# RetNet attention into a SiLU feed-forward block on one core: SiLU as one ScalarE operation, a shorter float64 conversion, an undecayed state, and a new order of the first and last groups

## Chip, core and metric

The kernel runs on one core of a Trainium2 chip. The metric is the device time of one execution in microseconds (us); lower is better. The engines are TensorE (PE, with its weight loads as PEld), VectorE (DVE), ScalarE (ACT), GpSimd (POOL) and SyncE (SP), whose queue issues nearly all DMAs.

## Reference

```python
# q, k, v: (4, 8, 768, 64) float32; w_in: (512, 2048), w_out: (2048, 512), float64
gamma = 1.0 - 2.0 ** (-5.0 - np.arange(H))
for t in range(S):
    state = gamma * state + einsum('bhd,bhe->bhde', k[:, :, t], v[:, :, t])
    y[:, :, t] = einsum('bhd,bhde->bhe', q[:, :, t], state) / sqrt(D)
x = y.transpose(0, 2, 1, 3).reshape(3072, 512)
h = x @ w_in
out = (h / (1 + exp(-h))) @ w_out          # SiLU, then the second product
```

## The kernel before

The sequence is cut into 6 **groups** `c` of 128 positions. A **unit** is the attention of one of the 4 batches in one group, with all 8 heads: 24 units in all. A unit has four stages. `stage_t` loads ahead, scales q (DVE, `qs`) and v (POOL, `vs`) by powers of gamma and transposes k and q on PE. `stage_a` makes the scores `sc` in two sets of 64-row matmuls (`j` = 0, 1, one for each half of the partitions) and masks them (`am`). `stage_y` adds the part from earlier groups (`y<-qt,state`) and the part from this group (`y<-am,vs`) in PSUM and splits the result into three fp32r parts of `xt`. `stage_s` makes the group's state update `s`, adds it to `state` and multiplies by the group's decay `gc`. The state of a head pair is kept as a 128x128 block with zeros off its diagonal, so that `y<-qt,state` has 128 rows of contraction and 64 output columns.

A **product** `product_in(c, f)` is one of 16 column blocks `f` of the first matrix product for group `c`: 12 matmuls of 512 columns into `ha` and `hb`; ACT scales `ha` into `hs` (L322), DVE subtracts `hb` (L323), ACT takes the sigmoid (L325), POOL multiplies (L326), and the result `g` goes to DRAM. PSUM holds two products at a time.

The weights are float64 in DRAM. `convert_w` makes float32 of them with integer operations on DVE: 8 per block (L158 to L173), of which five read one tensor and three read two. A block of `w_in` is then split in three (`split_w`: two ACT and two DVE operations); a converted block of `w_out` goes back to DRAM and is read and split later. `take_w` does one block.

Order of the first part: the units of group 0 with four blocks taken; then for each group all 16 products, each followed by one stage of the next group's attention. Group 0 takes a block after every product, the groups after it after one product in four. The second part (L409 to L411) then has 6 groups of 192 matmuls; its 16 blocks of `w_out` are read and split in its first group, two blocks ahead (`S_AHEAD`).

The calls are arranged on each engine's queue when the program is built; each queue then runs in that order, and an engine waits at its next instruction.

Of the kernel before, what the change touches and what calls it, by code (L numbers as in the profile page):

```python
# [12 lines left out]
FP32 = mybir.dt.float32  # L13
# [18 lines left out]
def kernel(  # L32
# [20 lines left out]

    nc = tc.nc
# [9 lines left out]
    assert S % C == 0 and NF == 4 * B  # L64
# [6 lines left out]
    dram = ctx.enter_context(tc.tile_pool(name="dram", bufs=1, space=bass.MemoryType.DRAM))  # L71
    wpool = ctx.enter_context(tc.tile_pool(name="wpool", bufs=1))
# [7 lines left out]
    def split_w(pool, f, w32, name):  # L80

        w = wpool.tile([128, 3, 512], FP32R, tag=f"w{f}", name=f"{name}{f}")
        lo = pool.tile([128, 512], FP32, tag="wl", name=f"{name}l_{f}")
# [9 lines left out]
    with ExitStack() as first:  # L93
        const = first.enter_context(tc.tile_pool(name="const", bufs=1))
        ld = first.enter_context(tc.tile_pool(name="ld", bufs=2))
        one = first.enter_context(tc.tile_pool(name="one", bufs=1))
        work = first.enter_context(tc.tile_pool(name="work", bufs=2))
        stage = first.enter_context(tc.tile_pool(name="stage", bufs=2))
        conv = first.enter_context(tc.tile_pool(name="conv", bufs=1))
        gp = first.enter_context(tc.tile_pool(name="gp", bufs=3))  # L100
        ps_a = first.enter_context(tc.tile_pool(name="ps_a", bufs=4, space=PS))
        ps_h = first.enter_context(tc.tile_pool(name="ps_h", bufs=2, space=PS))

        units = [(c, b) for c in range(NC) for b in range(B)]
        loaded = {}

        def load(n):
            if n >= len(units):
                return
            c, b = units[n]  # L110
            tiles = []
            for name, src in (("q", q), ("k", k), ("v", v)):
                t = ld.tile([128, H, D], FP32, tag=f"{name}f", name=f"{name}f_{n}")
                nc.sync.dma_start(out=t, in_=src[b, :, ds(c * C, C)].rearrange("h t d -> t h d"))
                tiles.append(t)
            loaded[n] = tiles
# [3 lines left out]
        staged = {}  # L120

        def load_w(i):
            if i >= 2 * NF:
                return
            if wide:
                t = stage.tile([128, 2 * DM], U32, tag="wf", name=f"wf_{i}")
                w_in, w_out, n = moe_w_in.bitcast(U32), moe_w_out.bitcast(U32), 256
            else:
                t = stage.tile([128, DM], FP32, tag="wf", name=f"wf_{i}")
                w_in, w_out, n = moe_w_in, moe_w_out, 128  # L130
            if i < NF:
                nc.sync.dma_start(out=t.rearrange("p (i f) -> p i f", i=KIN),
                                  in_=w_in[:, ts(i, n)].rearrange("(i p) f -> p i f", p=128))
            else:
                nc.sync.dma_start(out=t, in_=w_out[ts(i - NF, 128), :])
            staged[i] = t

        def convert_w(i):

            load_w(i + W_AHEAD)
            t = staged.pop(i)
            if not wide:  # L150
                return t
            words = t.rearrange("p (c w) -> p c w", w=2)
            lo, hi = words[:, :, 0], words[:, :, 1]
            a = conv.tile([128, DM], U32, tag="ca", name=f"ca_{i}")
            s = conv.tile([128, DM], U32, tag="cs", name=f"cs_{i}")
            p = conv.tile([128, DM], U32, tag="cp", name=f"cp_{i}")
            w = conv.tile([128, DM], FP32, tag="cw", name=f"cw_{i}")
            nc.vector.tensor_scalar(out=a, in0=hi, scalar1=0x7FFFFFFF, scalar2=None,  # L158
                                    op0=ALU.bitwise_and)
            nc.vector.tensor_scalar(out=a.bitcast(FP32), in0=a.bitcast(FP32),  # L160
                                    scalar1=bits((1151 << 20) - 1), scalar2=bits(896 << 20),
                                    op0=ALU.min, op1=ALU.max)
            nc.vector.tensor_scalar(out=a, in0=a, scalar1=4, scalar2=0x80000000,
                                    op0=ALU.logical_shift_left, op1=ALU.bitwise_xor)
            nc.vector.tensor_scalar(out=a, in0=a, scalar1=1, scalar2=None,
                                    op0=ALU.logical_shift_right)
            nc.vector.scalar_tensor_tensor(out=s, in0=hi, scalar=0x80000000, in1=a,  # L167
                                           op0=ALU.bitwise_and, op1=ALU.bitwise_or)
            nc.vector.tensor_scalar(out=p, in0=s, scalar1=0xFF800000, scalar2=None,
                                    op0=ALU.bitwise_and)  # L170
            nc.vector.scalar_tensor_tensor(out=p.bitcast(FP32), in0=lo, scalar=2.0 ** -52,
                                           in1=p.bitcast(FP32), op0=ALU.mult, op1=ALU.mult)
            nc.vector.tensor_tensor(out=w, in0=s.bitcast(FP32), in1=p.bitcast(FP32), op=ALU.add)  # L173
            return w

        w_sb = {}

        def take_w(i):
            if i >= 2 * NF:
                return  # L180
            w32 = convert_w(i)
            if i < NF:
                w_sb[i] = split_w(conv, i, w32, "wi")
            else:
                nc.sync.dma_start(out=wo_dram[i - NF], in_=w32)

        AHEAD = 2
        W_AHEAD = 2
        for n in range(max(AHEAD, W_AHEAD)):
            load(n)  # L190
            load_w(n)

        pos = const.tile([128, 1], FP32, tag="pos", name="pos")
        nc.gpsimd.iota(pos, pattern=[[0, 1]], base=1, channel_multiplier=1,
                       allow_small_or_imprecise_dtypes=True)
        ident = const.tile([128, 128], FP32, tag="ident", name="ident")
        make_identity(nc, ident)
        mask = const.tile([128, C], FP32, tag="mask", name="mask")
        nc.vector.memset(mask, 1.0)
        nc.gpsimd.affine_select(out=mask, in_=mask, compare_op=ALU.is_ge, fill=0.0,  # L200
                                base=0, pattern=[[1, C]], channel_multiplier=-1)
        lgp = const.tile([128, H], FP32, tag="lgp", name="lgp")
        for h in range(H):
            nc.vector.tensor_scalar(out=lgp[:, h : h + 1], in0=pos, scalar1=float(lg[h]),
                                    scalar2=None, op0=ALU.mult)
        gq = const.tile([128, H], FP32, tag="gq", name="gq")
        gk = const.tile([128, H], FP32, tag="gk", name="gk")
        nc.scalar.activation(out=gq, in_=lgp, func=AF.Exp)
        nc.scalar.activation(out=gk, in_=lgp, func=AF.Exp, scale=-1.0)
        nc.vector.tensor_scalar(out=gq, in0=gq, scalar1=scale, scalar2=None, op0=ALU.mult)  # L210
        gc = const.tile([128, HP, 1], FP32, tag="gc", name="gc")
        for a in range(HP):
            for j in range(2):
                nc.vector.memset(gc[ts(j, D), a, :], math.exp(C * lg[2 * a + j]))
        state = [const.tile([128, HP, 128], FP32, tag=f"state{b}", name=f"state{b}")
                 for b in range(B)]
        for st in state:
            nc.gpsimd.memset(st, 0.0)

        xt = {}  # L220
        live = {}

        def bank(name):
            return ps_a.tile([128, 512], FP32, tag="a", name=name)

        def stage_t(n):
            load(n + AHEAD)
            qf, kf, vf = loaded.pop(n)
            qs = one.tile([128, H, D], FP32, tag="qs", name=f"qs_{n}")
# [6 lines left out]
            for name, src in (("k", kf), ("q", qs)):  # L236
                tp = bank(f"{name}tp_{n}").rearrange("p (a t) -> p a t", a=HP)
                for a in range(HP):
                    nc.tensor.transpose(tp[:, a, :], src[:, 2 * a : 2 * a + 2, :], ident)
# [207 lines left out]
```

## Time and profile before

| | |
|---|---|
| median of 3 runs | 767.16 us (766.26 to 768.3) |
| the profiled execution | 766.99 us, of which the span from first to last instruction is 765.3 us |
| PE, PEld busy | 691.3 us (90%), 545.6 us (71%) |
| DVE, ACT, POOL busy | 518.8 (68%), 268.8 (35%), 159.9 us (21%) |
| granted PE clock | 0.953 of full speed over the span |
| DMA | 101.37 MB, 132 GB/s over the span |

A share is an average over parts of the kernel with different limits, so the parts are read apart. A busy PE says that a matmul was under way, not that PE ran at its best.

### The profile page before, as it was taken

The page shows a single profiled execution, that of the slowest core. Times are in us where ns is not written, and L with a number is a line of the kernel's source. Part 1 is how long each engine was busy: PE and PEld are TensorE (multiplying, and loading weights), DVE is VectorE, ACT ScalarE, POOL GpSimd, SP SyncE. Part 2 cuts the span into 40 slices and gives each one's busy share as a digit, 9 for nine tenths or more (in the row PEclk, how much of TensorE's full clock was granted, in tenths as well). Part 3 has the DMA queues.
Part 4 walks back from the last instruction along what each step waited for, and adds up shares of the span by engine and source line. Part 5 has one row for each costly group of instructions (what it writes and reads, how often), then busy time and mean ns, then how long its engine had stood idle before and what let it go on. Part 6 is the DMA issues. An engine that isn't in the chain of part 4 may idle for free.

```text
span 765.3 us, 10695 instructions
## 1 busy us (share of the span) xinstructions
PE 691.3 (90%) x3904; PEld 545.6 (71%) x3904; DVE 518.8 (68%) x842; ACT 268.8 (35%) x452; POOL 159.9 (21%) x132
## 2 busy tenths in 40 slices
PE   4599677779898889999999999699999999999997
PEld 3476345456676767777787888488888888888885
DVE  5989999999999995545554352298656555565653
ACT  2334323323333324433444344375323232232322
POOL 2113212223333333333333344300000000000000
PEclk9879968998999999999999999889999999999999
DMA  7745334356565544433342152364434334343431
GB/s 164 174 123 155 114 110 138 110 179 190 165 191 185 165 156 123 121 112 97 112 135 85 69 174 89 124 206 138 153 96 152 97 115 132 98 151 97 152 96 56
DMA packets 121397, 101.37 MB, mean 132 GB/s; under 512 B 79360, under 2 KB 87552, under 8 KB 121344
## 3 DMA queue, kind: packets, MB, share of 16 engines
q1 hardware_dynamic: 117888, 94.39, 41.5%
q10 hardware_dynamic: 3456, 6.29, 2.2%
q8 instruction: 31, 0.51, 0.3%
q14 instruction: 22, 0.18, 0.1%
HBM read 65.01 MB, written 35.65 MB: 132 GB/s over the span
## 4 chain that ended last, share of the span: by engine, by line
PE 60%; issue 16%; DVE 13%; POOL 7%; DMA 2%; ACT 1%; SPq 0%; POOLq 0%; DVEq 0%; ACTq 0%
PE oa L409 11%; PE oa L410 11%; PE ob L411 11%; POOL g L326 6%; PE ha L318 6%; PE hb L320 5%; PE ha L319 5%; PE y L274 3%; PE sc L250 2%; PE y L270 2%; DVE hs L323 2%; DVE am L256 1%; DVE cs L167 1%; DVE state L301 1%; PE s L292 1%
## 5 line engine op out<-in xcount | busy, mean ns | idle before, releaser
L326 POOL TENSOR_TENSOR g<-hs,g 128x512 f32<-128x512 f32 x96 | 131.4, 1369 | 248.0 <-ACT g L325 243.3
L318 PE MATMUL ha<-xt,wi 128*128 128x512 f32 x384 | 164.0, 428 | 15.1 <-ACT wi L84 13.5
L319 PE MATMUL ha<-xt,wi 128*128 128x512 f32 x384 | 158.2, 412 | 7.4 <-ACT wi L87 5.7
L320 PE MATMUL hb<-xt,wi 128*128 128x512 f32 x384 | 153.2, 414 | 4.3 <-DVE hs L323 3.5
L409 PE MATMUL oa<-wo,gs 128*128 128x512 f32 x384 | 150.2, 392 | 7.5 <-ACT wo L84 7.5
L410 PE MATMUL oa<-wo,gs 128*128 128x512 f32 x384 | 150.4, 392 | 0.0
L411 PE MATMUL ob<-wo,gs 128*128 128x512 f32 x384 | 150.3, 391 | 0.0
L387 DVE TENSOR_TENSOR gs<-gr,gs 128x512 fp32r<-128x512 f32 x96 | 66.0, 692 | 99.3 <-ACT gs L385 99.2
L323 DVE TENSOR_TENSOR hs<-hs,hb 128x512 f32<-128x512 f32 x96 | 65.7, 685 | 93.5 <-ACT hs L322 93.2
L385 ACT ACTIVATE gs<-gr 128x512 fp32r<-128x512 f32 x96 | 60.5, 632 | 168.0 <-PE ob L411 154.7
L318 PEld LDWEIGHTS ha<-xt,wi 128*128 128x128 f32 x384 | 74.6, 195 | 39.2 <-ACT wi L84 16.5
L322 ACT ACTIVATE hs<-ha 128x512 f32<-128x512 f32 x96 | 57.2, 596 | 126.1 <-PE ha L319 105.3
L325 ACT ACTIVATE g<-hs 128x512 f32<-128x512 f32 x96 | 60.7, 633 | 111.8 <-DVE hs L323 111.4
L319 PEld LDWEIGHTS ha<-xt,wi 128*128 128x128 f32 x384 | 75.6, 197 | 25.9 <-ACT wi L87 8.2
L320 PEld LDWEIGHTS hb<-xt,wi 128*128 128x128 f32 x384 | 75.0, 198 | 26.1 <-DVE hs L323 5.7
L409 PEld LDWEIGHTS oa<-wo,gs 128*128 128x128 f32 x384 | 72.6, 189 | 23.1 <-ACT wo L84 7.9
L410 PEld LDWEIGHTS oa<-wo,gs 128*128 128x128 f32 x384 | 72.7, 189 | 15.6 <-ACT wo L87 0.5
L411 PEld LDWEIGHTS ob<-wo,gs 128*128 128x128 f32 x384 | 72.6, 189 | 15.0
L388 DVE SCALAR_TENSOR_TENSOR gs<-gs 128x512 fp32r<-128x512 f32 x96 | 66.8, 700 | 2.4
L274 PE MATMUL y<-am,vs 128*64 128x128 f32 x384 | 50.5, 306 | 15.8 <-DVE am L256 15.4
L274 PEld LDWEIGHTS y<-am,vs 128*64 128x64 f32 x384 | 37.3, 154 | 22.2 <-issue 15.0
L233 POOL TENSOR_TENSOR vs<-vf,gk 128x512 f32<-128x512 f32 x24 | 25.9, 1079 | 83.0 <-PE y L274 39.3
(55 smaller groups left out, 671.8 us busy)
## 6 DMA issues: line engine op xcount, KB each, us to landing
gd<-g SPq DMA_DIRECT2D x96, 256.0 KB, 2.0
gr<-gd SPq DMA_DIRECT2D x96, 256.0 KB, 2.6
wf<-in_moe_w_in_dram SPq DMA_DIRECT2D x16, 512.0 KB, 3.9
wf<-in_moe_w_out_dram SPq DMA_DIRECT2D x16, 512.0 KB, 3.5
qf<-in_q_dram SPq DMA_DIRECT2D x24, 256.0 KB, 3.2
kf<-in_k_dram SPq DMA_DIRECT2D x24, 256.0 KB, 3.2
vf<-in_v_dram SPq DMA_DIRECT2D x24, 256.0 KB, 3.5
out_dram<-o ACTq DMA_DIRECT2D x24, 256.0 KB, 2.5
```

What stands on the lines that cost most here:

```text
L274: nc.tensor.matmul(yp[ts(j, D), a, :], lhsT=u["vs"][:, 2 * a + j, :], rhs=u["am"][j][:, a, :], start=(c == 0), stop=True, skip_group_check ...
L318: nc.tensor.matmul(ha, lhsT=w[0], rhs=x[0], start=first_, stop=False)
L319: nc.tensor.matmul(ha, lhsT=w[1], rhs=x[1], start=False, stop=last)
L320: nc.tensor.matmul(hb, lhsT=w[2], rhs=x[2], start=first_, stop=last)
L323: nc.vector.tensor_tensor(out=hs, in0=hs, in1=hb, op=ALU.subtract)
L325: nc.scalar.activation(out=g, in_=hs, func=AF.Sigmoid)
L326: nc.gpsimd.tensor_tensor(out=g, in0=hs, in1=g, op=ALU.mult)
L387: nc.vector.tensor_tensor(out=t[:, 1, :], in0=g, in1=high, op=ALU.subtract)
L388: nc.vector.scalar_tensor_tensor(out=t[:, 2, :], in0=t[:, 1, :].bitcast(FP32), scalar=-1.0 / EPS, in1=high, op0=ALU.mult, op1=ALU.add)
L409: nc.tensor.matmul(oa[b], lhsT=gh, rhs=wo[f][:, 0, :], start=first_, stop=False)
L410: nc.tensor.matmul(oa[b], lhsT=glo, rhs=wo[f][:, 1, :], start=False, stop=last)
L411: nc.tensor.matmul(ob[b], lhsT=gm, rhs=wo[f][:, 2, :], start=first_, stop=last)
```

## The change

SiLU is one ACT operation and POOL has no part in it. The conversion is one ACT operation (`Abs`, which also shifts the exponent by its scale) and six on DVE. The powers of gamma in `gq` and `gk` run on from position 0 through all groups (ten small POOL operations at the start, `chunk_decays`), so that the state needs no decay: it is only added to, as one 128x256 operation on dense 64x64 blocks, and for group 0 copied by ACT. `y<-qt,state` becomes a matmul of 64 rows and 64 columns. Groups 0 and 1 are done by halves of the column blocks, in the order (0, first half), (1, first half), (0, second), (1, second); `w_in` is taken over the first three of these, and group 1's and group 2's attention runs beside the first and the fourth, two stages per product. `w_out` is converted beside groups 2 and 3, and read and split during the products of group 5, in which the first `g` blocks of the second part are also loaded and split. All pools live through the program. Loads are issued with k first, then q and v.

```diff
-            nc.vector.tensor_scalar(out=a, in0=hi, scalar1=0x7FFFFFFF, scalar2=None,
-                                    op0=ALU.bitwise_and)
...
-            nc.vector.tensor_scalar(out=a, in0=a, scalar1=1, scalar2=None,
-                                    op0=ALU.logical_shift_right)
...
+        nc.scalar.activation(out=a.bitcast(FP32), in_=hi.bitcast(FP32), func=AF.Abs,
+                             scale=65536.0)
+        nc.vector.tensor_scalar(out=s, in0=hi, scalar1=0x80000000, scalar2=None,
+                                op0=ALU.bitwise_and)
+        nc.vector.tensor_scalar(out=a.bitcast(FP32), in0=a.bitcast(FP32),
+                                scalar1=bits(1024 << 20), scalar2=bits((1279 << 20) - 1),
+                                op0=ALU.max, op1=ALU.min)
+        nc.vector.scalar_tensor_tensor(out=s, in0=a, scalar=3, in1=s,
+                                       op0=ALU.logical_shift_left, op1=ALU.bitwise_or)
...
-                        nc.tensor.matmul(yp[ts(j, D), a, :], lhsT=state[b][:, a, ts(j, D)],
-                                         rhs=u["qt"][:, a, :], start=True, stop=False,
+                    nc.tensor.matmul(yp[ts(j, D), a, :], lhsT=state[b][ts(j, D), a, :],
+                                     rhs=u["qt"][ts(j, D), a, :], start=True, stop=False,
...
-                    nc.vector.tensor_tensor(out=st, in0=st, in1=src, op=ALU.add)
-                    src = st
-                nc.vector.tensor_tensor(out=st, in0=src,
-                                        in1=gc[ts(j, D)].to_broadcast([D, HP, D]), op=ALU.mult)
+        if c == 0:
+            nc.scalar.copy(out=state[b], in_=sp)
+        else:
+            nc.vector.tensor_tensor(out=state[b], in0=state[b], in1=sp, op=ALU.add)
...
-            nc.scalar.activation(out=g, in_=hs, func=AF.Sigmoid)
-            nc.gpsimd.tensor_tensor(out=g, in0=hs, in1=g, op=ALU.mult)
+        nc.scalar.activation(out=g, in_=hs, func=AF.Silu)
...
+    for c, f0 in ((0, 0), (1, 0), (0, half), (1, half)):
+        for i in range(half):
+            product_in(c, f0 + i)
+            if taken[0] < NF and (i < 5 if (c, f0) == (0, 0) else i % 2 == 0):
+                take_w()
+            put_g(1)
+            if (c, f0) == (0, 0) or (c, f0) == (1, half):
+                attend(c + 1, 2 * i)
+                attend(c + 1, 2 * i + 1)
+    for c in range(2, NC):
+        for f in range(NF):
+            product_in(c, f)
+            if c < NC - 1 and f % 2 == 1:
+                take_w()
+            put_g(1)
+            attend(c + 1, f)
+            if c == NC - 1:
...
+                wo[f] = split_w(f, w_got.pop(f), "wo")
+                get_w(f + 2)
...
+                    if f >= NF - S_AHEAD:
+                        split(f - NF + S_AHEAD)
```

Three places on the queues. First VectorE. Before, in group 0, these stand between the L323 of one product and that of the next (`wf` are the raw weights, `wil` is part of a split):

```order
L158 TENSOR_SCALAR ca_1254<-wf_1136 128x512
L173 TENSOR_TENSOR cw_1196<-cs_1194,cp_1195 128x512
L160 TENSOR_SCALAR ca_1254<-ca_1254 128x512
L299 TENSOR_TENSOR state_250<-state_250,s_1273 64x4x64
L163 TENSOR_SCALAR ca_1254<-ca_1254 128x512
L86 TENSOR_TENSOR wil_1206<-cw_1196,wi_1205 128x512
L165 TENSOR_SCALAR ca_1254<-ca_1254 128x512
L88 SCALAR_TENSOR_TENSOR wi_1205<-wi_1205,wil_1206 128x512
L167 SCALAR_TENSOR_TENSOR cs_1255<-wf_1136,ca_1254 128x512
L301 TENSOR_TENSOR state_250<-state_250,gc 64x4x64
L169 TENSOR_SCALAR cp_1256<-cs_1255 128x512
L299 TENSOR_TENSOR state_250<-state_250,s_1273 64x4x64
```

and now, in the first half of group 1 (`hs_1` and `hs_2` are two products in a row):

```order
L338 TENSOR_TENSOR hs_1_1151<-hs_1_1151,hb_1_1138 128x512
L175 TENSOR_TENSOR cw_1240<-cs_1238,cp_1239 128x512
L166 TENSOR_SCALAR ca_1296<-ca_1296 128x512
L164 TENSOR_SCALAR cs_1297<-wf_1176 128x512
L101 TENSOR_TENSOR wil_1249<-cw_1240,wi_1248 128x512
L338 TENSOR_TENSOR hs_2_1171<-hs_2_1171,hb_2_1158 128x512
```

Where one product shared VectorE with a whole conversion and state work, two products now share it with one shorter conversion.

Second TensorE, in `stage_y` of a unit of group 3, before, the first of its four head pairs:

```order
L270 MATMUL y_2639<-qt_2566,state_250 64x128 x2
L274 MATMUL y_2639<-am_14_2614,vs_2552 64x128
L274 MATMUL y_2639<-am_14_2616,vs_2552 64x128
```

and now, in a unit of group 4, the last two head pairs and what follows:

```order
L287 MATMUL y_3173<-qt_3103,state_244 64x128 x2
L291 MATMUL y_3173<-am_18_3149,vs_3089 64x128
L291 MATMUL y_3173<-am_18_3151,vs_3089 64x128
L287 MATMUL y_3173<-qt_3103,state_244 64x128 x2
L291 MATMUL y_3173<-am_18_3149,vs_3089 64x128
L291 MATMUL y_3173<-am_18_3151,vs_3089 64x128
L333 MATMUL ha_11_3193<-xt_2115,wi_1307 128x512
```

The rows stand in the same order, but L287 has 64 rows of contraction and L291 beside it 128, where L270 and L274 had 128 both: the shape now changes seven times within the `y` of a unit.

Third ScalarE in the products of group 5, before:

```order
L322 ACTIVATE hs_10_4321<-ha_10_4307 128x512
L325 ACTIVATE g_10_4324<-hs_10_4321 128x512
L322 ACTIVATE hs_11_4342<-ha_11_4328 128x512
L325 ACTIVATE g_11_4345<-hs_11_4342 128x512
L322 ACTIVATE hs_12_4363<-ha_12_4349 128x512
```

and now:

```order
L337 ACTIVATE hs_8_4192<-ha_8_4178 128x512
L99 ACTIVATE wo_4198<-wr_4148 128x512
L340 ACTIVATE g_8_4195<-hs_8_4192 128x512
L102 ACTIVATE wo_4198<-wol_4199 128x512
L337 ACTIVATE hs_9_4220<-ha_9_4206 128x512
```

Two operations per product have become four: both ACT parts of a `w_out` split stand between a product's operations and the next product's.

## Rows read from the trace of the kernel before

**Rows 1.** Stretch, length, busy us of PE, PEld, DVE, ACT, POOL; clock, DMA share, GB/s.
```profile
0.00:51.60 51.60, 29.26 (x252) 24.17 (x253) 38.81 (x89) 14.10 (x25) 8.06 (x17) 0.87 0.69 156
51.60:163.50 111.90, 85.32 (x471) 58.64 (x470) 106.63 (x184) 40.70 (x69) 28.52 (x19) 0.88 0.43 128
163.50:245.20 81.70, 73.51 (x477) 55.35 (x477) 78.94 (x131) 25.33 (x44) 26.64 (x21) 0.92 0.60 188
245.20:319.00 73.80, 69.68 (x482) 54.72 (x481) 58.24 (x89) 25.48 (x45) 26.99 (x21) 0.95 0.46 140
319.00:384.20 65.20, 65.20 (x482) 51.52 (x481) 34.59 (x52) 25.85 (x45) 24.91 (x20) 1.00 0.38 114
384.20:446.60 62.40, 62.40 (x420) 50.00 (x419) 28.07 (x40) 27.37 (x47) 22.70 (x19) 1.00 0.33 109
446.60:488.30 41.70, 41.70 (x179) 33.33 (x177) 12.98 (x18) 18.38 (x31) 20.29 (x16) 1.00 0.29 109
488.30:495.90 7.60, 0.16 (x1) 0.00 (x0) 0.69 (x1) 1.87 (x4) 1.82 (x2) 0.70 0.50 173
495.90:542.30 46.40, 46.36 (x193) 37.90 (x194) 39.53 (x64) 28.72 (x50) 0.00 (x0) 0.94 0.52 154
542.30:585.80 43.50, 43.50 (x194) 36.02 (x193) 24.16 (x38) 12.31 (x21) 0.00 (x0) 1.00 0.40 122
716.40:765.30 48.90, 43.63 (x193) 35.80 (x191) 23.59 (x36) 11.62 (x19) 0.00 (x0) 0.99 0.31 102
```

**Rows 2.** The instructions of L322 and L325: ns min/median/max, first and last start.
```profile
L322 ACT ACTIVATE hs<-ha x96: 577/598/605, 51.6 to 488.3; 128x512 f32<-128x512 f32 x96
L325 ACT ACTIVATE g<-hs x96: 615/632/653, 54.0 to 489.7; 128x512 f32<-128x512 f32 x96
```

**Rows 3.** Instructions of L163, L323, L301 and L326, as in rows 2.
```profile
L163 DVE TENSOR_SCALAR ca<-ca x32: 411/420/1520, 9.3 to 277.4; 128x512 uint32<-128x512 uint32 x32
L323 DVE TENSOR_TENSOR hs<-hs,hb x96: 672/689/690, 52.2 to 489.0; 128x512 f32<-128x512 f32 x96
L301 DVE TENSOR_TENSOR state<-state,gc x32: 409/422/1507, 78.4 to 384.2; 64x256 f32<-64x256 f32 x32
L326 POOL TENSOR_TENSOR g<-hs,g x96: 1262/1296/2933, 54.7 to 490.4; 128x512 f32<-128x512 f32 x96
```

**Rows 4.** Groups by line: busy us, mean ns; idle before them.
```profile
L301 DVE TENSOR_TENSOR state<-state,gc 64x256 f32<-64x256 f32 x32 | 25.3, 791 | 0.8
```

**Rows 5.** Timeline of PE around one `sc` in group 3: start, duration.
```profile
306.08 0.40 PE L320 MATMUL hb<-xt,wi 128*128 128x512 f32 x1
306.40 1.16 PE L250 MATMUL sc<-qt,kt 64*128 64x128 f32 x16
307.50 0.50 PE L318 MATMUL ha<-xt,wi 128*128 128x512 f32 x1
307.83 0.40 PE L319 MATMUL ha<-xt,wi 128*128 128x512 f32 x1
308.07 0.40 PE L320 MATMUL hb<-xt,wi 128*128 128x512 f32 x1
```

**Rows 6.** The same around one `y`.
```profile
310.50 0.44 PE L270 MATMUL y<-qt,state 128*64 128x128 f32 x4
310.77 0.39 PE L274 MATMUL y<-am,vs 128*64 128x128 f32 x4
310.99 0.39 PE L270 MATMUL y<-qt,state 128*64 128x128 f32 x4
...
312.08 0.39 PE L274 MATMUL y<-am,vs 128*64 128x128 f32 x4
312.40 0.51 PE L318 MATMUL ha<-xt,wi 128*128 128x512 f32 x1
```

**Rows 7.** Timeline where the second part starts; in brackets idle time and releaser.
```profile
495.26 1.23 ACT L84 ACTIVATE wo<-wr 128x512 fp32r<-128x512 f32 x2 [4.95 <-DMA wr<-wod]
495.94 0.80 PE L409 MATMUL oa<-wo,gs 128*128 128x512 f32 x1 [7.47 <-ACT wo L84]
```

More of the change, by code (lines that the diff above doesn't have):

```diff
@@ new lines, with load, load_w @@
+    units = [(c, b) for c in range(NC) for b in range(B)]
+    loaded = {}
+    def load(n):
+        if n >= len(units):
+            return
+        c, b = units[n]
+        tiles = []
+        for name, src in (("k", k), ("q", q), ("v", v)):
+            t = ld.tile([128, H, D], FP32, tag=f"{name}f", name=f"{name}f_{n}")
+            nc.sync.dma_start(out=t, in_=src[b, :, ds(c * C, C)].rearrange("h t d -> t h d"))
+            tiles.append(t)
+        loaded[n] = tiles
+    staged = {}
+    def load_w(i):
+        if i >= 2 * NF:
+            return
+        if wide:
+            t = stage.tile([128, 2 * DM], U32, tag="wf", name=f"wf_{i}")
+            w_in, w_out, n = moe_w_in.bitcast(U32), moe_w_out.bitcast(U32), 256
+        else:
+            t = stage.tile([128, DM], FP32, tag="wf", name=f"wf_{i}")
+            w_in, w_out, n = moe_w_in, moe_w_out, 128
+        if i < NF:
+            nc.sync.dma_start(out=t.rearrange("p (i f) -> p i f", i=KIN),
+                              in_=w_in[:, ts(i, n)].rearrange("(i p) f -> p i f", p=128))
+        else:
+            nc.sync.dma_start(out=t, in_=w_out[ts(i - NF, 128), :])
+        staged[i] = t
@@ L212, with stage_a @@
+    def stage_a(n):
+        u = live[n]
+        ap = [bank(f"sc{j}_{n}").rearrange("p (a t) -> p a t", a=HP) for j in range(2)]
         for a in range(HP):
             for j in range(2):
[L214 to L224, printed above, removed]
@@ new lines, in stage_s @@
+    def stage_s(n):
+        c, b = units[n]
+        u = live.pop(n)
+        if c == NC - 1:
+            return
+        sp = bank(f"s_{n}")[:, : HP * D].rearrange("p (a e) -> p a e", a=HP)
+        for a in range(HP):
+            for j in range(2):
+                h = 2 * a + j
+                nc.tensor.matmul(sp[ts(j, D), a, :], lhsT=u["kf"][:, h, :],
+                                 rhs=u["vs"][:, h, :], start=True, stop=True,
+                                 skip_group_check=True)
+        if c == 0:
+            nc.scalar.copy(out=state[b], in_=sp)
+        else:
+            nc.vector.tensor_tensor(out=state[b], in0=state[b], in1=sp, op=ALU.add)
@@ new lines, in put_g, with get @@
+    def put_g(keep):
+        while len(pending) > keep:
+            c, f, g = pending.pop(0)
+            nc.sync.dma_start(out=g_dram[c, f], in_=g)
+    order = [(c, f) for c in range(NC) for f in range(NF)]
+    got, ready, wo, w_got = {}, {}, {}, {}
+    def get(n):
+        if n >= len(order):
+            return
+        c, f = order[n]
+        g = ld.tile([128, NT], FP32, tag="kqv"[n % 3] + "f", name=f"gr_{c}_{f}")
+        nc.sync.dma_start(out=g, in_=g_dram[c, f])
+        got[n] = g
```

473 lines of the change are left out of this document (213 added, 260 removed).

## Prediction

> **What bounds the kernel now.** I read the busy times by stretch first [rows 1], cut where the first L322 of each group starts. The last two of these rows are the second part (its first group ends at 542.3, and three more like the 43.5 row lie between 585.8 and 716.4). The reader should look, row by row, for the engine that is busy nearly all the time.
>
> - Up to 245.2 us it is DVE: 106.63 of 111.90 and 78.94 of 81.70. PE is idle for 34.8 us of these 193.6, and its granted clock is 0.88 to 0.92, a mixture of 1.2 and 2.4 GHz, so some of its busy time is slow as well.
> - Group 2's stretch (73.8) is mixed. The next two (65.2 and 62.4) have PE busy throughout at clock 1.00: PE is the bound.
> - In group 5 PE is the bound with 41.7 for 15 products; then 7.6 us in which PE does nothing: it waits for ACT L84, which waited 4.95 us for the load of the first `w_out` block [rows 7].
> - The second part is PE's: 43.5 per group, 46.4 for the first, in which the clock is 0.94.
>
> So a gain has to come from DVE up to 245 us, from group 2's tail of that, or from the hand-over at 488 to 496.
>
> **DVE's work in the first two groups.** An undisturbed operation on 128x512 takes 0.42 us with one input tensor and 0.69 with two (medians of L163 and L323, [rows 3]). A conversion was five of the first kind and three of the second, 4.2 us; now three and three, 3.3. A block of `w_in` adds two for its split: 4.7. A unit is five of 0.69 (`qs`, two `am`, two `xt`), and the state, four operations of 0.42 before and one now (L301's size, [rows 3]): 3.9 us against 5.1. A product has one of 0.69.
>
> A second term is hidden in the durations. L301 has a median of 0.422 us and a mean of 0.791 [rows 3, 4], its maximum is 1.507, and L163, which should take 0.42 too, reaches 1.52. The excess of about 1.1 us is less than one POOL operation of 1.3 us (L326): some DVE operations are held while POOL runs. On L301 alone that is 32 x 0.37 = 11.8 us. With the SiLU in one ACT operation the 96 L326 go, and 24 smaller `vs` operations stay.
>
> By stage, for the new order (8 products each):
> - (0, first half) with group 1's units and five blocks: DVE 8 x 0.69 + 4 x 3.9 + 5 x 4.7 = 44.6.
> - (1, first) and (0, second) with four blocks: DVE 5.5 + 18.8 = 24.3 each.
> - (1, second) with group 2's units: DVE 5.5 + 15.6 = 21.1, and some `w_out` conversions drawn into it.
>
> **PE's work, and a new cost.** A product is 12 matmuls 0.234 apart (307.83 to 308.07, [rows 5]): 2.81 us. Group 3's 65.2 us less 16 x 2.81 leave 20.2 for four units, 5.05 each. Now look at how a matmul of another shape enters: 0.32 from 306.08 to 306.40 where 0.234 is normal, and 0.33 after the first product matmul that follows it [rows 5]. In the `y` of [rows 6] four records take 0.22, but 0.27 at the start, and 0.32 pass before the next product matmul. So a change into a 64-column shape costs about 0.09 + 0.05 = 0.15, one back to 128 columns 0.10 + 0.10 = 0.20. The new `y` changes between 64x64 and 128x64 seven times per unit. No row shows this very change. Bounds: 0, if these two shapes need no change, and 0.20 each; I take 0.15, the row with the same 64 columns: 7 x 0.15 = 1.05 us per unit, 21 us for the 20 units that have it, 28 by the upper bound. These units stand where PE is the bound, so all of it counts.
>
> The Trainium skill, "TensorEngine Tiling (Array Packing)", section Tiling Modes, speaks against this edit: a change of tiling mode, not of the tile alone, drains the array. The trace agrees for the changes that it has (0.32 for 0.234). The same section says that tiles work independently and in parallel. By that the two 64x64 matmuls of a head pair could overlap; a matmul is two records there and takes 0.11 (four records in 0.22, [rows 6]), so 4 x 0.11 x 20 = 9 us could come back. The sum has none of it, since the two halves of `sc` in [rows 5] take 1.10 us for 16 records, no less per record than a `y`.
>
> **The sum**, against the profiled span of 765.3:
> - Start to the first L322: 51.6 before. DVE has about 37 us to do from its first data (four conversions, three splits and a bit, four units without state) where it had some 45; I take 43.5. PE's first work waits for loads as before.
> - The 32 products of groups 0 and 1, 193.6 before. PE: 32 x 2.81 + 8 x 6.1 = 139. DVE is above PE in the two middle stages by 1.8 each. The clock was 0.92 where PE was 90% busy (163.5 to 245.2); half speed for a twentieth of the time adds 7. The queues hold each other up where both are full; I allow 4. Together 154.
> - Group 2: 73.8 becomes 65.2 + 4.2 = 69.4, since its DVE work (11 + 15.6 + 8 conversions of 3.3 = 53) is now below PE's. Group 3: 65.2 + 4.2 = 69.4. Group 4: 62.4 + 4.2 = 66.6.
> - Group 5: ACT has four operations per product instead of two, 0.60 + 3 x 0.63 = 2.49 ([rows 2]; a split's operation is of L325's size), against PE's 2.81, and four splits of the second part, 2.5 in all. They fit since `wo`'s first operation stands between `hs` and `g`, in the time that ACT waited for DVE. PE may have two products open, so a late ACT costs PE nothing until it is a product behind. I allow 1.5: 43.2.
> - Hand-over 7.6: 0.5, since the first blocks are split by then. First group of the second part 46.4: 43.5, without its slow clock. The rest is unchanged: 174.1 (542.3 to 716.4) and 48.9. The second part's splits now write into two blocks of four; a block is free when PE leaves it, 10.9 us before the next is needed, and four splits take at most 4 x (0.63 + 1.38) = 8.
>
> 43.5 + 154 + 69.4 + 69.4 + 66.6 + 43.2 + 0.5 + 43.5 + 174.1 + 48.9 = 713. The profiled execution took 766.99, 1.7 over its span and 0.2 under the median; so **715 us**, 7% less.
>
> **Rivals.**
> - *The shape change is free, or the 64x64 pairs overlap by as much as it costs.* For it: the columns stay 64, only the rows change. Against: `sc`, where only the rows are halved, pays. 715 - 21 = 694, and 685 if overlap is added.
> - *DVE and ACT hold each other up.* The conversion now starts on ACT, ACT also has `hs`, SiLU and two split operations, and each queue waits at its head; an `Abs` that waits for a load holds the `hs` behind it, and so PE. For it: both middle stages are within 2 us of balance. Against: ACT is busy 40.7 of 111.9 and gets only 0.63 per block more. If the first 32 products run at 180 instead of 154: 741.
> - *The last group runs as a chain.* If ACT waits for both DVE steps of a product instead of filling them (0.60 + 0.69 + 0.63 + 0.63 + 0.69 + 0.63 = 3.9 per product), group 5 takes 17 us more: 732.
> - *Slower.* The 64x64 matmuls lose the overlap of weight load and matmul altogether, because each goes to another corner of the array than the one before. The gain without the `y` term is 767 - 694 = 73 us; over 20 units that is 3.6 us per unit, or 0.23 for each of its 16 records of L287. From there on the change costs more than it gives. Four records that together take 0.22 of PE's time last 0.39 from the first start to the last end [rows 6], so each lasts far longer than its share of 0.055, and without any overlap such a price is possible: about 780. Against: the halves of `sc` alternate too and do not pay it.
> - *The contention stays*, because `vs` does it: 24 of 120 operations only, at most 8 x 1.1 = 9 us in the first 32 products. Inside the range.
>
> **Chances.** The forecast (700 to 730) 0.55, shape change free 0.22, DVE and ACT in each other's way 0.11, last group a chain 0.07, slower 0.05. For 8 in 10 the range needs the forecast, most of the free case and half of the third: 688 to 742. No change from 0.3% (2.3 us) either way, which is about what a measurement of this kernel can tell, needs the fourth rival at one price: 0.02. Faster 0.93, slower 0.05.
>
> **What would show it.** Right: no L326; DVE's integer operations with means at their medians; DVE below 95% from the second stage on; PE busy throughout from the middle of group 1; groups 2 to 4 at 66 to 70 us; seven starts of about 0.2 instead of 0.1 in each `y`; no gap before the second part. Wrong: `y` at its old 1.9 us (694), PE waiting for L99, L102 or L337 in the first halves (741) or in group 5 (732), or L287 records 0.3 apart (slower).

## The result, and the profile after

| | before | after |
|---|---|---|
| median | 766.71 us (4 runs, 765.25 to 768.3) | 692.45 us (4 runs, 690.54 to 695.33) |
| ratio, 95% interval | | 0.9034, 0.899 to 0.9078 |
| span of the profiled execution | 765.3 us | 691.5 us |
| PE busy | 691.3 us (90%) | 667.9 us (97%) |
| DVE, ACT, POOL busy | 518.8, 268.8, 159.9 us | 417.6, 279.4, 32.0 us |

The change is 9.7% faster. 715 us were forecast, with a range from 688 to 742; the time is 22.5 us below the forecast, near the 694 us of the rival that called the shape change free, whose mechanism the trace denies.

The busy times by stretch, which answer to [rows 1] (columns as there). The cuts are the starts of the first `hs` of a half group or group (L337, before L322), then of the first `oa` of a group:

```profile
0.00:44.90 44.90, 27.96 (x245) 24.27 (x245) 32.70 (x67) 18.18 (x35) 11.14 (x39) 0.85 0.80 184
44.90:92.10 47.20, 46.74 (x386) 34.46 (x386) 42.46 (x79) 27.94 (x48) 4.49 (x4) 1.00 0.65 177
92.10:113.80 21.70, 21.70 (x97) 17.97 (x96) 21.06 (x39) 15.02 (x27) 0.00 (x0) 1.00 0.60 183
113.80:135.80 22.00, 22.00 (x104) 18.03 (x104) 20.27 (x38) 15.17 (x28) 0.00 (x0) 1.00 0.65 206
135.80:181.60 45.80, 45.43 (x379) 32.98 (x377) 40.19 (x74) 19.96 (x36) 4.39 (x4) 1.00 0.76 229
181.60:249.50 67.90, 67.90 (x476) 50.15 (x475) 47.30 (x83) 28.80 (x50) 4.66 (x4) 1.00 0.62 193
249.50:317.90 68.40, 68.40 (x481) 50.69 (x480) 25.16 (x40) 25.88 (x44) 4.18 (x4) 1.00 0.38 108
317.90:383.40 65.50, 65.50 (x419) 49.26 (x418) 24.98 (x39) 27.78 (x48) 3.13 (x3) 1.00 0.35 107
383.40:423.80 40.40, 40.40 (x180) 33.46 (x179) 32.45 (x51) 34.50 (x61) 0.00 (x0) 1.00 0.72 214
423.80:467.30 43.50, 43.50 (x193) 36.05 (x192) 22.86 (x37) 12.02 (x22) 0.00 (x0) 1.00 0.33 109
```

From the first product on, PE is busy at least 99% of every row and its granted clock is 1.00, so it is at 2.4 GHz. The 32 products of groups 0 and 1, 193.6 us before, take 136.7. The cost of the new `y` is there; the timeline of PE around one `y`, beside [rows 6]:

```profile
256.85 0.39 PE L335 MATMUL hb<-xt,wi 128*128 128x512 f32 x1
257.17 0.43 PE L287 MATMUL y<-qt,state 64*64 64x128 f32 x4
257.53 0.44 PE L291 MATMUL y<-am,vs 128*64 128x128 f32 x4
...
259.74 0.44 PE L291 MATMUL y<-am,vs 128*64 128x128 f32 x4
260.11 0.50 PE L333 MATMUL ha<-xt,wi 128*128 128x512 f32 x1
```

Every four records now take 0.37 us where they took 0.22, and `y` takes 2.94 instead of 1.90 from its first start to the next product.

### The profile page after: what moved, and what is told of

It is laid out like the page before. It is cut to its first block, busy times and chain, and to the rows that moved or that the text cites. A ratio compares the mean times of both kernels' runs of the same rounds, so it can differ in the third digit from the quotient of the medians.

```text
span 691.5 us, 10415 instructions
## 1 busy us (share of the span) xinstructions
PE 667.9 (97%) x3904; PEld 527.2 (76%) x3904; DVE 417.6 (60%) x714; ACT 279.4 (40%) x488; POOL 32.0 (5%) x58
## 4 chain that ended last, share of the span: by engine, by line
PE 90%; DVE 4%; DMA 2%; ACT 1%; issue 1%; ACTq 0%; SPq 0%; DVEq 0%
PE ha L333 13%; PE oa L441 12%; PE oa L442 12%; PE ob L443 12%; PE ha L334 12%; PE hb L335 12%; PE y L291 5%; PE y L287 4%; PE sc L267 3%; DMA wf<-in_moe_w_in_dram 2%; PE s L309 1%; PE qtp L256 1%; PE ktp L256 1%; DVE am L273 1%; DVE cp L173 1%
## 5 line engine op out<-in xcount | busy, mean ns | idle before, releaser
L333 PE MATMUL ha<-xt,wi 128*128 128x512 f32 x384 | 155.8, 406 | 0.2 <-ACT xt L295 0.2
L334 PE MATMUL ha<-xt,wi 128*128 128x512 f32 x384 | 150.8, 393 | 0.0
L441 PE MATMUL oa<-wo,gs 128*128 128x512 f32 x384 | 148.8, 390 | 0.8 <-ACT o L447 0.8
L335 PE MATMUL hb<-xt,wi 128*128 128x512 f32 x384 | 149.2, 391 | 0.0
L442 PE MATMUL oa<-wo,gs 128*128 128x512 f32 x384 | 148.6, 389 | 0.0
L379 DVE TENSOR_TENSOR gs<-gr,gs 128x512 fp32r<-128x512 f32 x96 | 62.4, 685 | 91.8 <-ACT gs L377 91.8
L377 ACT ACTIVATE gs<-gr 128x512 fp32r<-128x512 f32 x96 | 53.4, 621 | 139.4 <-issue 128.7
L337 ACT ACTIVATE hs<-ha 128x512 f32<-128x512 f32 x96 | 56.8, 592 | 83.9 <-PE ha L334 82.7
L333 PEld LDWEIGHTS ha<-xt,wi 128*128 128x128 f32 x384 | 72.0, 188 | 18.2 <-issue 2.1
L334 PEld LDWEIGHTS ha<-xt,wi 128*128 128x128 f32 x384 | 72.2, 188 | 14.0
L380 DVE SCALAR_TENSOR_TENSOR gs<-gs 128x512 fp32r<-128x512 f32 x96 | 62.3, 684 | 0.4
L291 PE MATMUL y<-am,vs 128*64 128x128 f32 x384 | 46.1, 312 | 5.6 <-DVE am L273 5.4
L448 DVE TENSOR_TENSOR o<-o,ob 128x512 f32<-128x512 f32 x24 | 15.9, 686 | 40.8 <-ACT o L447 40.7
L291 PEld LDWEIGHTS y<-am,vs 128*64 128x64 f32 x384 | 23.3, 146 | 20.8 <-issue 19.8
```

The costliest lines, as they stand in the source:

```text
L291: nc.tensor.matmul(yp[ts(j, D), a, :], lhsT=u["vs"][:, 2 * a + j, :], rhs=u["am"][j][:, a, :], start=(c == 0), stop=True, skip_group_check ...
L333: nc.tensor.matmul(ha, lhsT=w[0], rhs=x[0], start=first_, stop=False)
L334: nc.tensor.matmul(ha, lhsT=w[1], rhs=x[1], start=False, stop=last)
L335: nc.tensor.matmul(hb, lhsT=w[2], rhs=x[2], start=first_, stop=last)
L337: nc.scalar.activation(out=hs, in_=ha, func=AF.Copy, scale=ONE_E)
L379: nc.vector.tensor_tensor(out=t[:, 1, :], in0=g, in1=high, op=ALU.subtract)
```

## Experiments

Twelve kernels. "After" is the changed kernel with its 692.45 us; intervals are those of the ratio to the kernel before, and "span" is that of the profiled execution.

| run | edit | median us | ratio, interval | span us |
|---|---|---|---|---|
| state128 | after, 128-row state | 674.72 | 0.8809, 0.8786 to 0.8831 | 670.3 |
| y_grouped | after, state matmuls first | 679.99 | 0.8870, 0.8853 to 0.8887 | 677.7 |
| paired | after, 128x128 matmuls in `y`, `s` | 686.01 | 0.8950, 0.8935 to 0.8965 | 684.3 |
| y_s_together | state128, `s` behind `y` | 672.62 | 0.8776, 0.8752 to 0.8800 | 674.1 |
| silu_only | before, SiLU alone | 728.10 | 0.9503, 0.9470 to 0.9537 | 727.5 |
| xt_shift32 | after, `xt` moved | 705.39 | 0.9196, 0.9176 to 0.9215 | 703.3 |
| before_xt_aligned | before, `xt` moved | 765.56 | 0.9986, 0.9965 to 1.0006 | 762.3 |
| silu_xt128 | silu_only, `xt` moved | 726.07 | 0.9466, 0.9447 to 0.9485 | 721.6 |
| group_order | after, old group order | 708.57 | 0.9230, 0.9196 to 0.9265 | 705.9 |
| old_conversion | after, old conversion | 694.22 | 0.9049, 0.9017 to 0.9082 | 691.2 |
| wout_second | after, split written later | 693.49 | 0.9026, 0.8987 to 0.9065 | 691.1 |
| wout_late | after, split held later | 701.11 | 0.9146, 0.9129 to 0.9164 | 698.6 |

### What the 64-row state costs: state128 and y_grouped

```diff
-                    nc.tensor.matmul(yp[ts(j, D), a, :], lhsT=state[b][ts(j, D), a, :],
-                                     rhs=u["qt"][ts(j, D), a, :], start=True, stop=False,
+                    nc.tensor.matmul(yp[ts(j, D), a, :], lhsT=state[b][:, a, ts(j, D)],
+                                     rhs=u["qt"][:, a, :], start=True, stop=False,
```

> The changed kernel with the state of a head pair kept as the 128x128 block with zeros that it was before, still without decay, so that the state's matmul in y has 128 rows again; two 64x256 additions per unit in place of one 128x256. Theory (each change between 64-row and 128-row matmuls costs PE about 0.15 us, seven in a unit): y falls from 2.9 to 1.9 us a unit and the time by 20 x 1.04 = 21, to about 671 us. Rival (the 64-row state costs the end nothing, y is covered by other waits): 690 to 694 us, although y is shorter.

```diff
-        for a in range(HP):
-            if c > 0:
+        if c > 0:
+            for a in range(HP):
                 for j in range(2):
...
-                                     rhs=u["qt"][ts(j, D), a, :], start=True, stop=False,
+                                     rhs=u["qt"][ts(j, D), a, :], start=(a == 0), stop=False,
...
+        for a in range(HP):
             for j in range(2):
                 nc.tensor.matmul(yp[ts(j, D), a, :], lhsT=u["vs"][:, 2 * a + j, :],
```

> The changed kernel with the 64-row state in another order within y: all eight state matmuls of a unit first, then all eight of am, so that the shape changes once instead of seven times between them. Theory (the cost hangs on the changes): six changes less, 6 x 0.15 = 0.9 us per unit and 18 in all, about 674 us. Rival (a 64x64 matmul is itself slow, 0.04 to 0.07 us per record more, whatever stands beside it): y stays at 2.7 to 2.9 us and the time at 688 to 693.

In state128 the addition to the state is also two operations of 64 rows again. The timelines of PE around one `y`, first state128, then y_grouped:

```profile
245.54 0.39 PE L339 MATMUL hb<-xt,wi 128*128 128x512 f32 x1
245.86 0.44 PE L289 MATMUL y<-qt,state 128*64 128x128 f32 x4
246.13 0.39 PE L293 MATMUL y<-am,vs 128*64 128x128 f32 x4
...
247.76 0.50 PE L337 MATMUL ha<-xt,wi 128*128 128x512 f32 x1
```

```profile
250.22 1.09 PE L287 MATMUL y<-qt,state 64*64 64x128 f32 x16
251.24 1.09 PE L292 MATMUL y<-am,vs 128*64 128x128 f32 x16
252.27 0.50 PE L334 MATMUL ha<-xt,wi 128*128 128x512 f32 x1
```

With 128 rows `y` is back at 1.90, and groups 2 to 4 take 63.5, 64.2 and 61.2 us, each 4.3 less: four units at 1.04. With 64 rows and one change inside `y` instead of seven, it takes 2.05: six changes less for 0.895, so 0.149 each. The 64x64 matmuls themselves are not slow: 16 records in 1.02 us, beside as many of 128x64 in 1.03. Both theories hold. The medians fall by 17.7 and 12.5 instead of 21 and 18, the spans by 21.2 and 13.8. In y_grouped groups 2, 3 and 4 give the full 3.6 or 3.7 each; the two stages that hold the units of groups 1 and 2 give 1.7 and 1.3. State128 gives 4.0 and 0.7 in these two, so how much of the price is on the path beside full VectorE work differs from stage to stage, and these runs do not say why.

### Wider matmuls, and s beside y: paired and y_s_together

```diff
+                nc.tensor.matmul(yp[:, a, :], lhsT=state[b][:, a, :], rhs=u["qt"][:, a, :],
+                                 start=(a == 0), stop=False, skip_group_check=True)
...
+            nc.tensor.matmul(sp[:, a, :], lhsT=u["kf"][:, 2 * a : 2 * a + 2, :],
+                             rhs=u["vs"][:, 2 * a : 2 * a + 2, :], start=True, stop=True,
```

> A version that may beat both: the changed kernel with the 128x128 state with zeros, used whole. In y four 128x128 matmuls per unit (one per head pair) come first, with no change of shape against the products, then the eight of am together; s is four 128x128 matmuls per unit over head pairs, of which the diagonal blocks are used. Theory (what PE pays here is matmuls and changes of shape): against state128's 674.7, y saves four matmuls, 4 x 0.10 = 0.4 us a unit, s about 0.3 (four of 0.11 for 0.615, and no change); 20 units, about 14 us: 660 us. Rival (the wider matmuls take as long as the pairs that they replace): 672 to 676.

The timeline of PE around a `y` and an `s` of paired:

```profile
259.08 0.39 PE L336 MATMUL hb<-xt,wi 128*128 128x512 f32 x1
259.31 1.05 PE L288 MATMUL y<-qt,state 128*128 128x128 f32 x8
260.29 1.09 PE L292 MATMUL y<-am,vs 128*64 128x128 f32 x16
...
264.17 1.05 PE L308 MATMUL s<-vs,kf 128*128 128x128 f32 x8
264.98 0.48 PE L334 MATMUL ha<-xt,wi 128*128 128x512 f32 x1
```

The rival was nearer, and for `y` it holds. In the trace the eight records of the four 128x128 matmuls start 0.11 us apart, 0.22 per matmul, as much as one of state128's pairs of 128x64; the 0.98 up to `am` holds one change of shape besides (0.21 behind the last of the eight). So `y` as a whole takes 2.01 instead of 1.90, with 0.09 saved at its start. `s` takes 0.81 instead of 0.61, since each of its matmuls now has 128 columns to move where it had 64. In groups 3 and 4, where PE sets the pace, paired takes 64.6 and 61.3 us, state128 64.2 and 61.2: nearly even. The 14 us between the two spans lie elsewhere: 5.8 arise before the first product (48.9 instead of 43.1) and 7.7 between it and group 3; neither was looked into.

```diff
-    stages = (stage_t, stage_a, stage_y, stage_s)
+    def stage_ys(n):
+        stage_y(n)
+        stage_s(n)
+    stages = (stage_t, stage_a, stage_ys, lambda n: None)
```

> A version that may beat all: state128 (128-row state, 674.7 us) with s issued right behind y in one stage, with no product between, since both have 128 rows and 64 columns. Theory (a way into this shape from a product costs 0.09 and the way back 0.10): 20 units save one of each, 3.8 us, about 670 to 671. Rival (the shorter unit leaves fewer products to hide the masks and the splits of the next one, so that waits of y for am or of ha for xt take it back): 674 to 678.

In its timeline `s` follows `y` at 0.22, without the 0.09 of a change, but the median is 2.1 below state128's and the two intervals overlap. PE waits 1.9 us for `xt` and 1.0 for `hs` in it, which state128 has at 0.7 and not at all. Which of the two is better is not settled; they beat the changed kernel by 2.6% and 2.9%.

### POOL's multiplication: silu_only

```diff
-nc.scalar.activation(out=g, in_=hs, func=AF.Sigmoid)
-nc.gpsimd.tensor_tensor(out=g, in0=hs, in1=g, op=ALU.mult)
+nc.scalar.activation(out=g, in_=hs, func=AF.Silu)
```

> The kernel before with one edit: SiLU in one ACT operation, no multiplication on POOL. Theory (POOL's multiplications held DVE operations, some 40 us in all, and DVE sets the pace in the first two groups): the mean of L301's operation falls from 0.79 to about 0.42 us, the two first groups shrink from 193.6 to about 165, the total to about 735. Rival (vs holds them, or it is no contention): L301 stays near 0.79 and the time at 760 to 767. On the interval of product matmuls, which stays misplaced by 32 bytes here: 0.234 if the placement sets it, 0.227 if POOL did.

Busy times of groups 0 and 1, beside [rows 1], then the group of L301, beside [rows 4]:

```profile
51.50:148.90 97.40, 80.96 (x471) 56.61 (x471) 91.65 (x182) 40.38 (x68) 4.62 (x4) 0.91 0.50 147
148.90:216.30 67.40, 65.18 (x476) 50.87 (x475) 66.06 (x135) 25.82 (x44) 4.30 (x4) 1.00 0.76 229
```

```profile
L301 DVE TENSOR_TENSOR state<-state,gc 64x256 f32<-64x256 f32 x32 | 13.4, 419 | 0.8
```

The same operation had a mean of 791 ns. DVE's busy time falls from 518.8 to 472.4 with the same 842 instructions, and the three stretches of groups 0 to 2 lose 14.5, 14.3 and 8.4 us: 37 of the 38 between the two spans. In groups 0 and 1 VectorE's busy time falls by 15.0 and 12.9, about as much, while the time that it is idle changes little (5.3 to 5.8 and 2.8 to 1.3). So the multiplications held VectorE, and the 24 `vs` that stay on POOL hardly do. Another path goes with them, ACT's waits for POOL to free an `hs` buffer (18.8 us in groups 0 and 1 before); that VectorE's idle time is as before says that they did not set the pace. The Trainium skill, "SBUF — State Buffer", section "SBUF: two separate sides", says that VectorE and GpSimd share one pair of ports as an exclusive lock held for the whole instruction. The trace agrees: L163 and L301, with all inputs in SBUF, stretch to 1.5 us, by 1.1 where an L326 takes 1.3, while L323, which reads one input from PSUM, never exceeds 690 ns [rows 3]. It does not catch every such operation: L86 reads two inputs from SBUF and stays below 0.70 us in all its 16 on `w_in`. This edit alone thus gives half of the gain.

### Why product matmuls became faster: xt_shift32, before_xt_aligned, silu_xt128

Product matmuls follow each other faster than before. The experiments move `xt` in SBUF by an unused tile ahead of its pool (`work` in the kernel before; 8 words are 32 bytes per partition, 24 are 96). The pools behind it move too: with `xt` in the two kernels made from the one before, and by 64 bytes in xt_shift32, where a second such tile, not shown here, stands behind `xpool`. The other operand of the product matmuls, `wi`, stays where it was in all of them.

```diff
+    gap = pool("gap", 1)
+    gap.tile([128, 8], FP32, tag="gap", name="gap")
     xpool = pool("xpool", 2)
```

> The changed kernel with the two xt buffers alone moved by 32 bytes in SBUF, so that they start at 32 modulo 64 as in the kernel before, where they now start at 0. Theory A (the start of the moving rows sets the interval of product matmuls, 0.2267 us now and 0.2342 before): 0.234 again in the first part, 1152 x 0.0075 = 8.6 us more, about 701 us, the second part unchanged at 0.2267, since its moving rows are wo. Theory B (POOL's 96 multiplications slowed the matmuls before): no change, 690 to 695 us, 0.2267.

> The kernel before with xt and hs moved by 32 bytes, so that xt starts at 0 modulo 64; nothing else. Theory (a start at 32 costs each product matmul 7 ns, which counts only where PE sets the pace): interval 0.227 in all of the first part; groups 0 and 1 stay at 194, since DVE sets their pace, groups 2 to 5 lose 768 x 0.0075 = 5.8, about 761 us. Rival (the interval comes from something else in the changed kernel, and the shift there hurt in another way): 767, 0.234.

> The kernel before with SiLU in one operation (as in silu_only) and xt moved by 96 bytes, so that it starts at 0 modulo 128. So far 0 modulo 128 had 0.2267 us between product matmuls, 32 and 64 modulo 128 had 0.233 to 0.234. Theory A (0 modulo 128 is what counts): 0.227 in the first part, and since PE sets the pace from group 1 on, about 7 us less than silu_only's 728, 720 to 722. Theory B (not the start of xt, but something else that the changed kernel has): 0.234 and 726 to 730.

Two L318, L337 or L320 twelve matmuls apart, in silu_only (32 modulo 128), xt_shift32 (32), before_xt_aligned (64) and silu_xt128 (0):

```profile
447.56 0.40 PE L318 MATMUL ha<-xt,wi 128*128 128x512 f32 x1
...
450.37 0.39 PE L318 MATMUL ha<-xt,wi 128*128 128x512 f32 x1
```

```profile
409.70 0.40 PE L337 MATMUL ha<-xt,wi 128*128 128x512 f32 x1
...
412.50 0.40 PE L337 MATMUL ha<-xt,wi 128*128 128x512 f32 x1
```

```profile
475.77 0.40 PE L320 MATMUL ha<-xt,wi 128*128 128x512 f32 x1
...
478.57 0.40 PE L320 MATMUL ha<-xt,wi 128*128 128x512 f32 x1
```

```profile
438.55 0.39 PE L320 MATMUL ha<-xt,wi 128*128 128x512 f32 x1
...
441.27 0.39 PE L320 MATMUL ha<-xt,wi 128*128 128x512 f32 x1
```

2.81, 2.80, 2.80 and 2.72 us. Two of the three slow ones have no multiplication on POOL, so it is not POOL; the first guess, a start at a multiple of 64 bytes, fell with the third; at 0 modulo 128, where the changed kernel's `xt` stands too, the interval is 0.227. In xt_shift32 the second part slows as well, which theory A did not expect:

```profile
427.90:472.70 44.80, 44.80 (x193) 36.06 (x192) 22.89 (x37) 12.02 (x22) 0.00 (x0) 1.00 0.34 106
```

There the moving rows (`wo`) stay where they were and the weights (`gs`, in the `xt` buffers) are shifted. So such a start of either operand costs up to 7 ns per matmul (44.8 instead of 43.5 for 192); the whole was 12.9 us. That this is near theory A's 8.6 is in part luck: 7.7 us of it lie in the second part, and between the first `hs` and the first `oa` only 4.3 (383.3 instead of 379.0): 0.9 in the 32 products of groups 0 and 1, 0.7 in each of groups 2 to 4, and the full 1.3 only in group 5, which has no attention beside it. The trace shows why: in after the product matmuls are about 0.23 us apart for the first eight or so behind an attention stage and 0.227 only from there on, 0.229 to 0.230 on average in groups 2 to 4, while in xt_shift32 it is 0.233 everywhere. In the total time the two other kernels show little: before_xt_aligned kept its interval and its time (0.8 us less than the runs of before beside it, inside the error), and silu_xt128 is 2.0 below silu_only by the medians and 5.9 by the spans, where 7 were expected. The interval is settled for the starts tried (0, 32 and 64), the gain in total only bounded.

### The order of groups and the conversion: group_order and old_conversion

```diff
-    for c, f0 in ((0, 0), (1, 0), (0, half), (1, half)):
...
+    for c in range(2):
+        for f in range(NF):
+            product_in(c, f)
+            if taken[0] < NF:
+                take_w()
+            put_g(1)
+            attend(c + 1, f)
```

> The changed kernel with groups 0 and 1 in the order of before: all 16 products of group 0 with a block of w_in after each until all are taken and one stage of group 1's attention, then group 1. Theory (the halves spread w_in's DVE work under PE's): in group 0 DVE has 13 x 4.7 + 16 x 0.69 + 4 x 3.9 = 88 us against 68 of PE, so the 32 products take 88 + 68 = 156 instead of 136.7 and the total is about 711 us, with PE idle again behind L99 and L102. Rival (with the contention gone and the conversion shorter, the order is worth nothing): 690 to 696.

The stretches of groups 0 and 1, then two of PE's waits (us in total, times, longest):

```profile
45.10:126.80 81.70, 74.40 (x474) 52.05 (x473) 75.04 (x140) 47.30 (x81) 4.23 (x4) 0.98 0.56 162
126.80:195.20 68.40, 68.40 (x481) 50.71 (x480) 57.28 (x104) 32.50 (x55) 4.18 (x4) 1.00 0.75 237
```

```profile
PE ha L333 <- ACT wi L99: 4.2, 4, 1.6
PE ha L334 <- ACT wi L102: 2.1, 3, 0.9
```

The theory holds in kind: 16.1 us in the median, 13.4 of them in these two stretches (150.1 instead of 136.7, where 156 were expected), and PE waits for the splits of `w_in` again. DVE was 75 us busy where 88 were worked out, mostly for a reason that comes below.

```diff
-        nc.scalar.activation(out=a.bitcast(FP32), in_=hi.bitcast(FP32), func=AF.Abs,
-                             scale=65536.0)
+        nc.vector.tensor_scalar(out=a, in0=hi, scalar1=0x7FFFFFFF, scalar2=None,
+                                op0=ALU.bitwise_and)
...
```

> The changed kernel with the conversion of before: eight operations on DVE, none on ACT. DVE gets 0.9 us more per block, ACT 0.67 less. Theory (the conversion is near DVE's limit in the first three stages, where DVE is busy 83.8 of 90.9 us): 11 blocks there add 10 us, of which 7 fit, and the middle stages go from 21.8 to 23.5; 695 to 700 us. Rival 1 (all hidden): 692. Rival 2 (the Abs on ACT was what held L337): faster than 690.

1.8 us more, with intervals that overlap: rival 1, nearly all hidden. The 32 products of groups 0 and 1 take 138.7 us instead of 136.7, and the start before them is 1.7 shorter. In the third half group, into which more of the attention was drawn, VectorE has come level with PE:

```profile
111.80:143.70 31.90, 30.42 (x188) 23.08 (x187) 30.72 (x60) 15.34 (x27) 1.04 (x1) 1.00 0.57 173
```

It is no proof that the shorter conversion is worth nothing in the old order, where DVE sets the pace; that was not tried.

### The hand-over: wout_second and wout_late

```diff
     def split(n):
...
+        if c == 0:
+            wo[f] = split_w(f, w_got.pop(f), "wo")
+            get_w(f + 2)
...
-                wo[f] = split_w(f, w_got.pop(f), "wo")
-                get_w(f + 2)
```

> The changed kernel with w_out read and split as before in the first group of the second part, and the first three g blocks split after the last product; everything else stays. Theory (the split in group 5 saves the wait at the hand-over and the slow clock behind it): the second part starts some 7 us later and its first group takes 46 instead of 43.5, about 702 us; group 5's products stay at 40.4, since PE sets their pace. Rival (queues run ahead, so the first block is split in time anyway): 690 to 695.

No change (1.0 us, with intervals that overlap), and the groups of ACT in group 5 say why:

```profile
L102 ACT ACTIVATE wo<-wol 128x512 fp32r<-128x512 f32 x15 | 9.5, 633 | 0.5 <-DVE wol L101 0.5
L99 ACT ACTIVATE wo<-wr 128x512 fp32r<-128x512 f32 x15 | 9.3, 623 | 0.5 <-DMA wr<-wod 0.5
```

The code now has the splits in the second part, but 15 of the 16 stand in group 5 all the same, as in after: nothing held the loads, and the arrangement of the queues drew them forward. The next kernel holds them by a buffer:

```diff
-            t = stage.tile([128, DM], FP32, tag="wf", name=f"wr_{f}")
+            t = hpool.tile([128, DM], FP32, tag="hs", name=f"wr_{f}")
```

> wout_second again, but with the raw w_out blocks in the two hs buffers, which come free only with the last two SiLUs, so that no block can be read and split during group 5: in wout_second the code said the second part, and the queues had 15 of the 16 splits in group 5 all the same. Theory (the hand-over's wait is that of a buffer which the last products hold): first block's load after the last SiLU, 2 to 3 us, and a split operation of 0.63, so oa starts 5 to 7 us after the last product, and the first group takes 46 instead of 43.5: 700 to 704 us. Rival (the wait before was made by something else, such as the DMA queue behind POOL's last g): 692 to 696.

Its timeline at the hand-over, beside [rows 7], then the stretch of the second part's first group, beside [rows 1]:

```profile
427.86 0.63 ACT L99 ACTIVATE wo<-wr 128x512 fp32r<-128x512 f32 x1 [1.86 <-DMA wr<-wod]
428.54 1.65 PE L444 MATMUL oa<-wo,gs 128*128 128x512 f32 x3 [6.13 <-ACT wo L99]
```

```profile
428.50:474.70 46.20, 46.16 (x193) 37.75 (x194) 36.89 (x58) 25.38 (x44) 0.00 (x0) 0.94 0.52 160
```

The old picture is back: 6.1 us idle, the clock at 0.94 in the group behind, and 8.7 us in the median. What ends the wait is a buffer that comes free early enough, not the place in the code. Whether in the kernel before the closed pools or the last `g` in the DMA queue held the load was not tried.

## Why the prediction was right or wrong

The sum, stage by stage:

| term | forecast | measured |
|---|---|---|
| start to first `hs` | 43.5 | 44.9 |
| 32 products of groups 0 and 1 | 154 | 136.7 |
| groups 2, 3, 4 | 69.4, 69.4, 66.6 | 67.9, 68.4, 65.5 |
| group 5 and hand-over | 43.7 | 40.4 |
| second part | 266.5 | 267.7 |

- **The bound, and POOL's contention: right.** Removing POOL's multiplications alone gave 39 us, and restoring the old order cost 16 us with DVE's work in PE's way.
- **The range: in part luck.** 700 to 730 was the forecast proper. The room below 700 stood there for a free shape change, which did not come; other terms brought the time into it.
- **The shape change: right.** 1.05 us per unit forecast, 1.04 measured; in full on the path in groups 2 to 4, in part beside groups 0 and 1. The rival at 694 us said that it is free; its time came out by other terms, not by its mechanism. The rival by which 64x64 matmuls lose all overlap (780) is denied by y_grouped.
- **The term that was mis-sized: 154 for the first 32 products.** The forecast was 138.7 of PE's work, 14.6 of allowances and 0.7 of rounding. Of the 17.3 us too many, 14.6 are the three allowances (3.6 for DVE above PE, 7 for the clock, 4 for queues), and all three were nothing: PE is busy 135.87 of 136.7 us at clock 1.00. Their common ground was DVE at 24.3 us in each middle stage; it was busy 21.06 and 20.27. So the sign "DVE below 95% from the second stage on" failed in the second (97% of 21.7 us), and still PE did not wait. Durations were added as if one operation ended before the next began. A piece of DVE's timeline of after:

```profile
95.08 0.68 DVE L338 TENSOR_TENSOR hs<-hs,hb 128x512 f32<-128x512 f32 x1
95.68 0.68 DVE L175 TENSOR_TENSOR cw<-cs,cp 128x512 f32<-128x512 f32 x1
96.28 0.41 DVE L166 TENSOR_SCALAR ca<-ca 128x512 f32<-128x512 f32 x1
96.62 0.42 DVE L164 TENSOR_SCALAR cs<-wf 128x512 uint32<-128x512 uint32 x1
```

  Operations that last 0.68 start 0.60 apart, and 0.34 behind one of 0.41: an operation that needs nothing from the one ahead of it, and waits for no other engine, starts about 0.08 before its end. One that needs it does not: L171, which reads what L169 ahead of it wrote, starts 0.03 after its end. In the two middle stages the durations add up to 23.8 and 22.9 us, so the overlap is 2.7 and 2.6; the rest of the 24.3 is an operation or two that ran in another stage. The overlap puts DVE below PE's 21.7.
- **The matmul interval, 0.234: mis-sized.** It was taken as fixed, but `xt` stands elsewhere. At 0.0075 a matmul this would be 2.9 us of the first 32 products (384 matmuls) and 1.4 of each later group. By xt_shift32, which puts the old start back, it is 0.9 of the 2.0 us by which PE's own work was too large there, and 0.7 of the 1.0 to 1.5 that are missing in each of groups 2 to 4. The rest of both is open.
- **Group 5 and hand-over: right in kind.** ACT is busy 34.5 of 40.4 and PE never waits for it; the 1.5 allowed were not needed. That the hand-over goes, since the first blocks are split by then, is right: `oa` follows the last product without a gap, and 15 of the 16 blocks are split in group 5. It is not the new place in the code that does it, as wout_second shows.
- **The other rivals** show no trace: after has no wait of PE for L99, L102 or L337, and its longest sum of waits is 5.4 us, of `y` for `am`.
- **Open.** The start is 6.7 us shorter. It is not the SiLU (51.5 in silu_only) nor the conversion (43.2 in old_conversion); load order and state were not tried apart. The single gains measured by one edit each do not add up to the whole; that order, conversion and contention all relieve the same DVE may be why, but was not tested.

## What to carry to other kernels

Before engines are weighed against each other, read how far apart their back-to-back instructions start, not how long they last: durations made VectorE look 13% fuller than it was in the two middle stages (23.8 us for 21.06, 22.9 for 20.27). A smaller matmul is no saving where it changes the array's shape between its neighbours; put equal shapes together, or keep the zeros. What frees a stage is the buffer or engine that holds it, so check in the trace that an edit of the code's order has moved anything.

## What the runs showed of the hardware

- A change between 64x64 and 128x64 matmuls costs 0.149 us of PE, within the bounds of 0 and 0.20. The Trainium skill, "TensorEngine Tiling (Array Packing)", section Tiling Modes, has the drain, and the runs agree; a pair of 128x64 matmuls takes 0.22 us, as much as one 128x128 with the same 128 columns to move (paired), as its rule of independent tiles lets expect.
- The start of `xt` in SBUF modulo 128 bytes sets the interval of 512-column matmuls: 0.227 us at 0 (0.23 for the first few behind an attention stage), 0.233 to 0.234 at 32 and 64. Other starts were not tried.
- VectorE starts an operation about 0.08 us before the end of the one ahead where it needs nothing from it and waits for no other engine; where it needs its result, 0.03 after that end (L171 behind L169).
